# Three edits in an attention kernel: the causal mask of the row maxima, v's scale, v's low part

## The chip, the cores and the metric

The kernel runs on one core of a Trainium2 chip. The metric is the device time of one execution in microseconds. Three executions of the kernel before took 941.6, 941.88 and 940.47 us; the median is 941.6.

## The reference

Three parts follow each other. The sizes are 4 batches, 8 heads, 576 positions and 64 columns a head; the model width is 512.

```
# 1: attention with decay, per head
scores = q k^T / 8 + cum[i] - cum[j]          # cum: running sum of log f
scores[j > i] = -1e9;  scores -= max over j
attn = exp(scores);  attn /= sum + 1e-9
x = attn @ v                                  # heads side by side: 512 columns
# 2: low-rank mixing over positions, then a feed-forward block
u = x + (x^T @ U @ V)^T
x = u + relu(u @ w1) @ w2                     # w1 512x2048, w2 2048x512
# 3: four attention experts, the best two of each position weighted
logits = x @ w_gate;  w = softmax of the two largest, 0 for the others
out = sum over e of w[e] * (causal_softmax(x wq[e] (x wk[e])^T / 8) @ (x wv[e])) @ wo[e]
```

## The kernel before

Keys lie on the 128 partitions of a score tile and queries on its columns, so the row maximum cannot be had from that tile. The maxima are computed beforehand by matmuls of their own (`row_max`, one call per head): "ua" holds the last 128 queries against all 576 keys, "ub" the other four query tiles against the 64, 192, 320 and 448 keys that they may see. The last 128 keys of each (64 in the smallest) are the diagonal block, where the causal mask has to be applied: VectorE adds the mask tile maskm and takes the maximum in one operation per query tile (lines 158 and 176), in place in PSUM. The four operations of ub need all four of its matmuls, which stand together. The five columns are transposed on TensorE ("mt", line 181), shifted ("mr", line 183) and sent by two DMAs of the SP queue into row 66 of qa, from where the score matmuls subtract them.

`scores` makes the score tiles in three-term precision (qa with ka, qb with kb) and masks the diagonal blocks on TensorE: identb times maskt is added to the bank (the last matmuls of line 212). ScalarE takes the exponential (pf, line 221) and its fp16 part ph (line 222), VectorE the rest pl (line 223). `weighted_values` multiplies ph and pl with v's high part vh and low part vl; a column of constants beside vh gives the row sums, and `row_scales` divides.

v needs a scale before it is split in two fp16 parts. `value_scale` takes the largest absolute value of each partition on VectorE (am, line 250), then the largest of all partitions by a transpose on TensorE (amt) and a reduce (ar, line 255), keeps its power of two (two small operations), and sends it back to all partitions by a product with ones (rsp) and a reciprocal (rs, line 264). It is a generator: its callers place its pieces among other work. `value_parts` multiplies v in place on VectorE (vr, line 269), casts it to vh on ScalarE (line 270) and subtracts on GpSimd to get vl (line 271). The tile vr is loaded again two pairs later.

The program's order: the 32 heads of part 1 are 16 pairs. Pairs 0 to 3 (batch 0) run without other matmuls beside them, up to about 90 us. From pair 5 on, between about 120 and 420 us, every turn of a pair also takes some groups of the feed-forward matmuls of batches already done (GROUPS: 6, 6, 7, then 8 a pair). From 420 to 711 us the rest of the feed-forward runs alone. From 711 us on come the experts: 16 heads in four batches, with the projections of the next batch beside them. In a turn of pair p stand the scores of p, the maxima and v's scale of pair p + 1, and the loads of pair p + 2. The order on TensorE is written out by hand; the other engines' orders come from the framework, which simulates a timeline. SP's DMA queue is in order. w1 and w2 come in quarters through `narrow` (lines 307 to 310, VectorE and ScalarE) and a subtraction on GpSimd (line 345); GpSimd also makes the low parts of q and k (qb and kb, lines 519 to 522) and of u (ul, line 356). In part 3, `gates` (eq, gt, gex and others, VectorE) is put behind the instruction that `value_parts` returns.

Maxima of pair 0 are made at the start, and those of pair p + 1 in the turn of pair p; the 14 heads of pairs 0 to 6 have their ua between 11.6 and 154.6 us.

Of the kernel before, what the change touches and what calls it, by code (L numbers as in the profile page):

```python
# [8 lines left out]
F32 = mybir.dt.float32  # L9
# [8 lines left out]
P = 128  # L18
# [13 lines left out]
AUG = 67  # L32
NH2A = 2
# [25 lines left out]
def kernel(  # L59
# [51 lines left out]
    ones1 = const.tile([1, P], BF16, name="ones1")  # L111
    nc.gpsimd.memset(ones1[:], 1.0)
# [37 lines left out]
    def row_max(hb, mx, apart=False):  # L150
# [4 lines left out]
        for c0, c1 in ((0, HC), (HC, S)):  # L155
            nc.tensor.matmul(ua[:, c0 // HC, 0:HC], qa[0:66, M_LO[4]:S], ka[0:66, c0:c1],  # L156
                             start=True, stop=True)
        nc.vector.tensor_tensor_reduce(
            ua[:, :, 0:HC], ua[:, :, 0:HC],
            maskm[:].rearrange("p (c n) -> p c n", c=2), 1.0, NEG, OP.add, OP.max, mx[:, 4:5])  # L160
# [4 lines left out]
        for t in (3, 2, 1, 0):  # L165
            bk, off = where[t]
            w = M_W[t]
            n = 64 if t == 0 else P
            nc.tensor.matmul(ub[0:n, bk, off:off + w], qa[0:66, M_LO[t]:M_LO[t] + n],  # L169
                             ka[0:66, 0:w], start=True, stop=True)  # L170
        for t in (3, 2, 1, 0):
            bk, off = where[t]
            w = M_W[t]
            n = 64 if t == 0 else P
            m0 = S - P if t == 0 else S - w
            nc.vector.tensor_tensor_reduce(  # L176
                ub[0:n, bk, off:off + w], ub[0:n, bk, off:off + w], maskm[0:n, m0:m0 + w], 1.0, NEG,
                OP.add, OP.max, mx[0:n, t:t + 1])
# [68 lines left out]
    def value_scale(vr):  # L247

        am = small.tile([P, 1], F32, name="am")
        nc.vector.tensor_reduce(am[:], vr, AX.XYZ, OP.max, apply_absolute_value=True)  # L250
        yield
        at_ = psf.tile([1, P], F32, name="amt", tag="f")
        nc.tensor.transpose(at_[:], am[:], ident[:])
        ar = small.tile([1, 1], F32, name="ar")
        nc.vector.tensor_reduce(ar[:], at_[:], AX.X, OP.max)
        nc.vector.tensor_scalar(ar[:], ar[:], 1.0e-30, None, OP.max)
        nc.vector.tensor_scalar(ar[:].bitcast(I32), ar[:].bitcast(I32), 0x7F800000, None,
                                OP.bitwise_and)
        yield

        rp = psf.tile([P, 1], F32, name="rsp", tag="f")
        nc.tensor.matmul(rp[:], ones1[:], ar[:].bitcast(BF16)[:, 1:2], start=True, stop=True)
        rs = small.tile([P, 1], F32, name="rs")
        nc.vector.reciprocal(rs[:], rp[:])
        return rs

    def value_parts(vr, rs, vh, vl):

        scaled = nc.vector.tensor_scalar(vr, vr, rs[:, 0:1], VEXP, OP.mult, OP.mult)
        nc.scalar.copy(vh[:, :, :, 0:64], vr)  # L270
        nc.gpsimd.tensor_tensor(vl[:], vr, vh[:, :, :, 0:64], OP.subtract)
        return scaled

    def row_scales(av, rs, extra=None):
# [3 lines left out]
                                1.0e-9 * PSCALE * VEXP, rs[:, 0:1], OP.add, OP.mult)  # L278
# [192 lines left out]
    for i in range(2):  # L471
        vh_ = hpool.tile([P, 2, NT, 65], F16, name=f"vh{i}")
        vl_ = hpool.tile([P, 2, NT, 64], F16, name=f"vl{i}")
        nc.gpsimd.memset(vh_[:, :, :, 64:65], VEXP)
        vhs.append((vh_, vl_))
# [55 lines left out]
    def maxima(p, j, apart=False):  # L531
        if p < NPAIR:
            yield from row_max(pair_heads(p)[j], next_mx(), apart)
# [347 lines left out]
    def expert_values(b, y):  # L881
# [18 lines left out]
        nc.gpsimd.memset(vh[:, :, :, 64:65], VEXP)  # L900
# [213 lines left out]
```

## Time and profile before

| | |
|---|---|
| median of 3 executions | 941.6 us (940.47 to 941.88) |
| profiled execution, first to last instruction (span) | 939.0 us |
| TensorE busy | 847.3 us, 90% |
| VectorE busy | 562.3 us, 60% |
| ScalarE busy | 415.3 us, 44% |
| GpSimd busy | 294.1 us, 31% |
| mean granted clock of TensorE | 0.954 |

The span is that of one profiled execution; the page gives no time before its first and behind its last instruction. PE is TensorE, PEld its weight loads, DVE VectorE, ACT ScalarE, POOL GpSimd, SP the queue that issues most DMAs. L176 is line 176. A line such as "ub<-ub,maskm 128x448" names the output, the inputs and the shape (partitions x columns). "Idle before" is time in which the engine stood still ahead of such instructions, with what ended it. The granted clock is a share of full speed: 1.0 is 2.4 GHz, 0.5 is 1.2 GHz.

### The profile page before, as it was taken

Reading aid. Unit: us, or ns where it says so; the run is one execution under the profiler, and the core shown is the slowest. Engines: PE = TensorE matmul, PEld = TensorE weight load, DVE = VectorE, ACT = ScalarE, POOL = GpSimd, SP = SyncE. Lnnn points to the kernel's source line nnn. Section 1 sums busy time; section 2 is a strip of 40 time slices with the busy share of each in tenths; the row PEclk is TensorE's granted clock in tenths of the full one; section 3 lists DMA queues with packets and bytes.
Section 4 is the critical chain, followed back from the end, with each engine's and each line's share of the span. In section 5 each row is a group of like instructions: output and inputs, shape, how many; then the busy total and the mean of one; then the engine's idle time right before and its main releaser. Section 6 shows DMA issues by size and latency. Waiting matters only on the chain.

```text
span 939.0 us, 18998 instructions
## 1 busy us (share of the span) xinstructions
PE 847.3 (90%) x7480; PEld 792.6 (84%) x7480; DVE 562.3 (60%) x1468; ACT 415.3 (44%) x808; POOL 294.1 (31%) x262
## 2 busy tenths in 40 slices
PE   2886878999899989989998999999999897989897
PEld 2775767888899989989998999999999797978675
DVE  6798588787576657632256652222225778786653
ACT  4675546564445463332233342222113464644553
POOL 8545354353423333012135433323014131210100
PEclk9998567999999999999999999999999998989998
DMA  6345545353433341103178753424114130311222
GB/s 190 106 108 163 141 149 166 112 146 114 126 109 86 111 136 47 39 15 114 53 267 262 233 185 113 152 74 121 37 29 124 39 90 17 91 29 27 70 85 69
DMA packets 68777, 101.94 MB, mean 109 GB/s; under 512 B 6608, under 2 KB 49424, under 8 KB 68688
## 3 DMA queue, kind: packets, MB, share of 16 engines
q1 hardware_dynamic: 64416, 92.47, 33.4%
q10 hardware_dynamic: 4272, 8.26, 2.5%
q8 instruction: 59, 0.97, 0.4%
q14 instruction: 30, 0.25, 0.1%
HBM read 60.33 MB, written 22.56 MB: 88 GB/s over the span
## 4 chain that ended last, share of the span: by engine, by line
PE 70%; DVE 14%; DMA 6%; ACT 5%; issue 3%; POOL 1%; SPq 1%; POOLq 0%; ACTq 0%; DVEq 0%
PE cps L385 19%; PE hps L370 19%; PE sc L212 8%; PE pq L849 4%; PE po L935 3%; PE pv L892 3%; PE av L239 3%; DVE pl L223 2%; DMA ust<-udram 2%; PE ub L169 2%; DVE ub L176 2%; PE gp L552 2%; PE av L243 2%; PE av L241 2%; PE ua L156 1%
## 5 line engine op out<-in xcount | busy, mean ns | idle before, releaser
L385 PE MATMUL cps<-hh,w2h 128*128 128x288 f32 x512 | 155.4, 304 | 6.8 <-DVE yc L387 3.8
L223 DVE TENSOR_TENSOR pl<-pf,ph 128x576 f16<-128x576 f32 x144 | 121.6, 847 | 54.4 <-ACT ph L222 54.2
L385 PE MATMUL cps<-hh,w2l 128*128 128x288 f32 x512 | 152.2, 297 | 1.0 <-POOL w2l L345 1.0
L370 PE MATMUL hps<-uh,w1h 128*128 128x288 f32 x512 | 145.2, 305 | 6.7 <-ACT uh L355 6.7
L385 PE MATMUL cps<-hl,w2h 128*128 128x288 f32 x512 | 151.2, 295 | 0.0
L370 PE MATMUL hps<-uh,w1l 128*128 128x288 f32 x512 | 141.9, 299 | 0.0
L375 DVE SCALAR_TENSOR_TENSOR hl<-hps,hh 128x288 fp32r<-128x288 f32 x128 | 58.2, 455 | 127.3 <-ACT hh L374 127.1
L374 ACT ACTIVATE hh<-hps 128x288 fp32r<-128x288 f32 x128 | 52.3, 409 | 168.6 <-PE hps L370 168.4
L221 ACT ACTIVATE pf<-sc 128x576 f32<-128x576 f32 x144 | 83.6, 612 | 52.3 <-PE sc L212 48.6
L385 PEld LDWEIGHTS cps<-hh,w2h 128*128 128x128 f32 x512 | 97.1, 190 | 8.3 <-DVE yc L387 4.5
L370 PEld LDWEIGHTS hps<-uh,w1h 128*128 128x128 f32 x512 | 97.9, 191 | 7.2 <-ACT uh L355 7.2
L370 PEld LDWEIGHTS hps<-uh,w1l 128*128 128x128 f32 x512 | 98.0, 191 | 0.0
L385 PEld LDWEIGHTS cps<-hh,w2l 128*128 128x128 f32 x512 | 96.9, 189 | 1.2 <-POOL w2l L345 1.2
L385 PEld LDWEIGHTS cps<-hl,w2h 128*128 128x128 f32 x512 | 96.9, 189 | 0.0
L370 PE MATMUL hps<-ul,w1h 128*128 128x288 f32 x512 | 89.6, 297 | 3.2 <-POOL ul L356 3.2
L212 PE MATMUL sc<-qa,ka 67*128 67x288 f32 (+4 forms) x288 | 79.1, 334 | 14.6 <-DMA qa<-mr 5.5
L222 ACT CAST ph<-pf 128x576 f16<-128x576 f32 x144 | 88.7, 638 | 1.6
L239 PE MATMUL av<-vh,ph 128*128 128x65 f16 x720 | 86.4, 202 | 1.5 <-DVE x L286 1.5
L176 DVE CUSTOM_DVE_ANT_0 ub<-ub,maskm 128x448 f32<-128x448 f32 x192 | 81.4, 424 | 7.2 <-PE ub L169 6.0
L241 PE MATMUL av<-vl,ph 128*128 128x64 f16 x720 | 85.1, 198 | 0.0
L243 PE MATMUL av<-vh,pl 128*128 128x65 f16 x720 | 84.8, 198 | 0.0
L356 POOL TENSOR_TENSOR ul<-ust,uh 128x1152 fp32r<-128x1152 f32 x22 | 58.8, 2671 | 80.9 <-ACT uh L355 80.9
(160 smaller groups left out, 1984.9 us busy)
## 6 DMA issues: line engine op xcount, KB each, us to landing
raw<-in_w_dram SPq DMA_DIRECT2D x32, 512.0 KB
ust<-udram SPq DMA_DIRECT2D x22, 576.0 KB
qkt<-in_qk_dram SPq DMA_DIRECT2D x16, 576.0 KB
yc<-ydram SPq DMA_DIRECT2D x14, 576.0 KB
ydram<-yc SPq DMA_DIRECT2D x14, 576.0 KB
vr<-in_v_dram SPq DMA_DIRECT2D x16, 320.0 KB
udram<-ustage ACTq DMA_DIRECT2D x16, 288.0 KB
ydram<-ust SPq DMA_DIRECT2D x8, 576.0 KB
```

The source lines that it names most:

```text
L176: nc.vector.tensor_tensor_reduce(ub[0:n, bk, off:off + w], ub[0:n, bk, off:off + w], maskm[0:n, m0:m0 + w], 1.0, NEG, OP.add, OP.max, mx[0 ...
L212: nc.tensor.matmul(ps[:, bk, off:off + w], wa, xa, start=bk not in banks[:n], stop=bk not in banks[n + 1:])
L221: nc.scalar.activation(pfv, view, AF.Exp, scale=ISC)
L222: nc.scalar.copy(ph[:, o0:o0 + n], pf[:, 0:n])
L223: nc.vector.tensor_tensor(pl[:, o0:o0 + n], pf[:, 0:n], ph[:, o0:o0 + n], OP.subtract)
L239: nc.tensor.matmul(av[0:m, it, :], ph[0:k, c:c + m], vh[0:k, jt, :], start=first, stop=False)
L241: nc.tensor.matmul(av[0:m, it, 0:64], ph[0:k, c:c + m], vl[0:k, jt, :], start=False, stop=False)
L243: nc.tensor.matmul(av[0:m, it, :], pl[0:k, c:c + m], vh[0:k, jt, :], start=False, stop=last)
L356: nc.gpsimd.tensor_tensor(ul[:], ust[:], f32(uh[:]), OP.subtract)
L370: nc.tensor.matmul(ph[:], wa[:, k, fs], xa[:, k, :], start=n == 0, stop=n == 3 * KT - 1)
L375: nc.vector.scalar_tensor_tensor(hl[:], ph[:], 0.0, f32(hh[:]), OP.max, OP.subtract)
L385: nc.tensor.matmul(pc[:], wa[:, t, dsl], xa[:], start=n == 0, stop=n == 3 * FT - 1)
```

## The change

For the heads of pairs 0 to 6 (PLAIN = 7) the mask of the maxima is added on TensorE: identb times the diagonal columns of maskm, one matmul for ua and four for ub, behind the products in the same bank; VectorE then takes a plain maximum of each query tile. The other heads, those of part 3 too, keep the fused operation.

v's scale is one product: the partition maxima, now bf16, with a 128x128 tile of ones. Their sum over the partitions stands in for the largest of them; VectorE scales it by 1/8192, takes the power of two and the reciprocal. The column of constants beside vh is 1.0 and no longer 8192.

v is no longer scaled in place: ScalarE multiplies by rs and casts in one pass, and vl is one VectorE operation, v times rs minus vh. `value_parts` returns this last operation.

```diff
@@ -30,6 +30,7 @@
 NQ = 4
 FT = FF // P // NQ
 AUG = 67
+PLAIN = 7
 NH2A = 2
 NH2B = 4
 PSCALE_LN = 8.0 * math.log(2.0)
@@ -108,8 +109,8 @@
                             compare_op=OP.is_ge, fill=BIG, base=0, channel_multiplier=1)
 
 
-    ones1 = const.tile([1, P], BF16, name="ones1")
-    nc.gpsimd.memset(ones1[:], 1.0)
+    every = const.tile([P, P], BF16, name="every")
+    nc.gpsimd.memset(every[:], 1.0)
 
     def make_heads(pl_, n, decay):
 
@@ -147,17 +148,22 @@
             except StopIteration as end:
                 return end.value
 
-    def row_max(hb, mx, apart=False):
+    def row_max(hb, mx, apart=False, onpe=False):
 
 
         qa, qb, ka, kb = hb
         ua = ps2.tile([P, 2, 512], F32, name="ua", tag="s2")
         for c0, c1 in ((0, HC), (HC, S)):
             nc.tensor.matmul(ua[:, c0 // HC, 0:HC], qa[0:66, M_LO[4]:S], ka[0:66, c0:c1],
-                             start=True, stop=True)
-        nc.vector.tensor_tensor_reduce(
-            ua[:, :, 0:HC], ua[:, :, 0:HC],
-            maskm[:].rearrange("p (c n) -> p c n", c=2), 1.0, NEG, OP.add, OP.max, mx[:, 4:5])
+                             start=True, stop=c0 == 0 or not onpe)
+        if onpe:
+            nc.tensor.matmul(ua[:, 1, HC - P:HC], identb[:], maskm[:, S - P:S], start=False,
+                             stop=True)
+            nc.vector.tensor_reduce(mx[:, 4:5], ua[:, :, 0:HC], AX.XY, OP.max)
+        else:
+            nc.vector.tensor_tensor_reduce(
+                ua[:, :, 0:HC], ua[:, :, 0:HC],
+                maskm[:].rearrange("p (c n) -> p c n", c=2), 1.0, NEG, OP.add, OP.max, mx[:, 4:5])
         if apart:
             yield
         ub = ps2.tile([P, 2, 512], F32, name="ub", tag="s2")
@@ -167,12 +173,21 @@
             w = M_W[t]
             n = 64 if t == 0 else P
             nc.tensor.matmul(ub[0:n, bk, off:off + w], qa[0:66, M_LO[t]:M_LO[t] + n],
-                             ka[0:66, 0:w], start=True, stop=True)
+                             ka[0:66, 0:w], start=not onpe or t > 1, stop=not onpe)
+        for t in (0, 3, 2, 1) if onpe else ():
+            bk, off = where[t]
+            n = 64 if t == 0 else P
+            off += M_W[t] - n
+            nc.tensor.matmul(ub[0:n, bk, off:off + n], identb[0:n, 0:n],
+                             maskm[0:n, S - P:S - P + n], start=False, stop=t in (1, 3))
         for t in (3, 2, 1, 0):
             bk, off = where[t]
             w = M_W[t]
             n = 64 if t == 0 else P
             m0 = S - P if t == 0 else S - w
+            if onpe:
+                nc.vector.tensor_reduce(mx[0:n, t:t + 1], ub[0:n, bk, off:off + w], AX.X, OP.max)
+                continue
             nc.vector.tensor_tensor_reduce(
                 ub[0:n, bk, off:off + w], ub[0:n, bk, off:off + w], maskm[0:n, m0:m0 + w], 1.0, NEG,
                 OP.add, OP.max, mx[0:n, t:t + 1])
@@ -246,36 +261,30 @@
 
     def value_scale(vr):
 
-        am = small.tile([P, 1], F32, name="am")
+        am = small.tile([P, 1], BF16, name="am")
         nc.vector.tensor_reduce(am[:], vr, AX.XYZ, OP.max, apply_absolute_value=True)
         yield
-        at_ = psf.tile([1, P], F32, name="amt", tag="f")
-        nc.tensor.transpose(at_[:], am[:], ident[:])
-        ar = small.tile([1, 1], F32, name="ar")
-        nc.vector.tensor_reduce(ar[:], at_[:], AX.X, OP.max)
-        nc.vector.tensor_scalar(ar[:], ar[:], 1.0e-30, None, OP.max)
-        nc.vector.tensor_scalar(ar[:].bitcast(I32), ar[:].bitcast(I32), 0x7F800000, None,
+        sp = psf.tile([P, 1], F32, name="rsp", tag="f")
+        nc.tensor.matmul(sp[:], every[:], am[:], start=True, stop=True)
+        rs = small.tile([P, 1], F32, name="rs")
+        nc.vector.tensor_scalar(rs[:], sp[:], 1.0 / VEXP, 1.0e-30, OP.mult, OP.max)
+        nc.vector.tensor_scalar(rs[:].bitcast(I32), rs[:].bitcast(I32), 0x7F800000, None,
                                 OP.bitwise_and)
+        nc.vector.reciprocal(rs[:], rs[:])
         yield
-
-        rp = psf.tile([P, 1], F32, name="rsp", tag="f")
-        nc.tensor.matmul(rp[:], ones1[:], ar[:].bitcast(BF16)[:, 1:2], start=True, stop=True)
-        rs = small.tile([P, 1], F32, name="rs")
-        nc.vector.reciprocal(rs[:], rp[:])
         return rs
 
     def value_parts(vr, rs, vh, vl):
 
-        scaled = nc.vector.tensor_scalar(vr, vr, rs[:, 0:1], VEXP, OP.mult, OP.mult)
-        nc.scalar.copy(vh[:, :, :, 0:64], vr)
-        nc.gpsimd.tensor_tensor(vl[:], vr, vh[:, :, :, 0:64], OP.subtract)
-        return scaled
+        nc.scalar.mul(vh[:, :, :, 0:64], vr, rs[:, 0:1])
+        return nc.vector.scalar_tensor_tensor(vl[:], vr, rs[:, 0:1], vh[:, :, :, 0:64], OP.mult,
+                                              OP.subtract)
 
     def row_scales(av, rs, extra=None):
 
         den = small.tile([P, NT], F32, name="den")
         nc.vector.tensor_scalar(den[:], av[:, :, 64:65].rearrange("p t o -> p (t o)"),
-                                1.0e-9 * PSCALE * VEXP, rs[:, 0:1], OP.add, OP.mult)
+                                1.0e-9 * PSCALE, rs[:, 0:1], OP.add, OP.mult)
         rn = small.tile([P, NT], F32, name="rn")
         nc.vector.reciprocal(rn[:], den[:])
         if extra is not None:
@@ -471,7 +480,7 @@
     for i in range(2):
         vh_ = hpool.tile([P, 2, NT, 65], F16, name=f"vh{i}")
         vl_ = hpool.tile([P, 2, NT, 64], F16, name=f"vl{i}")
-        nc.gpsimd.memset(vh_[:, :, :, 64:65], VEXP)
+        nc.gpsimd.memset(vh_[:, :, :, 64:65], 1.0)
         vhs.append((vh_, vl_))
     NPAIR = B * NP
     st_in, st_rs, st_p = {}, {}, {}
@@ -530,7 +539,7 @@
 
     def maxima(p, j, apart=False):
         if p < NPAIR:
-            yield from row_max(pair_heads(p)[j], next_mx(), apart)
+            yield from row_max(pair_heads(p)[j], next_mx(), apart, p < PLAIN)
 
     def one(gen):
 
@@ -897,7 +906,7 @@
                 yield
         vh = sy.tile([P, NT, E, 65], F16, name="vh3")
         vl = sy.tile([P, NT, E, 64], F16, name="vl3")
-        nc.gpsimd.memset(vh[:, :, :, 64:65], VEXP)
+        nc.gpsimd.memset(vh[:, :, :, 64:65], 1.0)
         vv_ = vr[:, :, 0:E * D].rearrange("p t (e d) -> p t e d", e=E)
         scale = value_scale(vv_)
         next(scale)
```

## Rows read from the trace of the kernel before

**Rows 1.** Each engine's busy us in four stretches: A:B, length, engines, clock, DMA

```profile
0.00:160.00 160.00, 114.72 (x979) 99.32 (x980) 123.25 (x320) 91.04 (x162) 85.47 (x88) 0.83 0.50 144
87.00:132.00 45.00, 32.83 (x200) 28.34 (x201) 29.43 (x62) 21.16 (x38) 21.31 (x13) 0.51 0.51 155
160.00:420.00 260.00, 247.05 (x2476) 228.63 (x2474) 172.88 (x482) 128.98 (x246) 87.21 (x64) 0.98 0.33 97
711.00:939.00 228.00, 199.32 (x1884) 179.57 (x1882) 155.68 (x445) 116.23 (x248) 32.98 (x36) 0.95 0.23 61
```

**Rows 2.** Chain of waits, 0 to 160 us: shares of 160 us by line

```profile
by line: PE sc L212 14.0%; issue 9.9%; DVE pl L223 6.6%; DMA qa<-mr 4.6%; DVE wst L307 4.5%; DVE ub L176 4.5%; ACT pf L221 3.8%; PE ub L169 3.7%; DMA qkt<-in_qk_dram 2.9%; ACT ph L222 2.7%; PE av L239 2.7%; PE gp L552 2.5%; DVE ua L158 2.4%
```

**Rows 3.** Chain of waits, 711 to 939 us: shares of 228 us

```profile
by line: PE pq L849 16.6%; PE po L935 12.8%; PE sc L212 10.4%; PE pv L892 10.4%; DVE pl L223 3.8%; DVE ub L176 3.4%; PE av L239 3.4%; DVE am L250 2.6%; PE ub L169 2.6%; PE av L243 2.2%; PE av L241 2.2%; DMA yst<-ydram 2.0%; DVE eq L819 2.0%
```

**Rows 4.** TensorE in order of time near 44 and 50 us: start, us

```profile
43.95 0.58 PE L212 MATMUL sc<-maskt,identb 128*128 128x64 bf16 x4
44.32 0.42 PE L181 MATMUL mt<-ident,mx 128*5 128x128 f32 x1
...
50.48 0.37 PE L212 MATMUL sc<-maskt,identb 128*128 128x64 bf16 x4
50.69 0.27 PE L181 MATMUL mt<-ident,mx 128*5 128x128 f32 x1
```

**Rows 5.** Groups by line, 0 to 160 us: busy us, mean ns, idle before

```profile
L176 DVE CUSTOM_DVE_ANT_0 ub<-ub,maskm 128x448 f32<-128x448 f32 (+3 forms) x56 | 23.8, 425 | 3.4 <-PE ub L169 3.0
...
L169 PE MATMUL ub<-ka,qa 66*128 66x448 f32 (+3 forms) x56 | 13.7, 384 | 3.8 <-DVE mx L158 3.1 <-ACT pf L221 0.7
...
L158 DVE CUSTOM_DVE_ANT_0 ua<-ua,maskm 128x576 f32<-128x576 f32 x14 | 10.6, 759 | 5.5 <-PE ua L156 5.5
...
L176 DVE DVE_READ_ACCUMULATOR2_ANT mx<- 128x1 f32 (+1 forms) x56 | 7.6, 136 | 0.0
...
L250 DVE TENSOR_REDUCE am<-vr 128x1 f32<-128x640 f32 x7 | 5.7, 810 | 3.0 <-DMA vr<-in_v_dram 3.0
...
L270 ACT CAST vh<-vr 128x640 f16<-128x640 f32 x7 | 5.1, 727 | 4.3 <-DVE vr L269 4.3
...
L269 DVE TENSOR_SCALAR vr<-vr,rs 128x640 f32<-128x640 f32 x7 | 4.3, 621 | 0.0
...
L255 DVE TENSOR_REDUCE ar<-amt 1x1 f32<-1x128 f32 x7 | 1.9, 273 | 1.3 <-PE amt L253 1.3
```

**Rows 6.** Line 309 of the whole span: shortest, median, longest ns

```profile
L309 DVE SCALAR_TENSOR_TENSOR wst<-raw,wst x32: 675/693/2699, 76.4 to 560.0; 128x512 int32<-128x512 int32 x32
```

**Rows 7.** VectorE, GpSimd and TensorE in order of time, 83 to 92 us

```profile
86.92 1.83 DVE L223 TENSOR_TENSOR pl<-pf,ph 128x512 f16<-128x512 f32 x1
...
88.81 1.75 DVE L309 SCALAR_TENSOR_TENSOR wst<-raw,wst 128x512 int32<-128x512 int32 x1
...
86.79 1.41 POOL L271 TENSOR_TENSOR vl<-vr,vh 128x640 f16<-128x640 f32 x1
88.28 1.73 POOL L522 TENSOR_TENSOR kb<-qkt,kb 64x576 fp32r<-64x576 f32 x1
...
91.03 0.58 PE L561 MATMUL up<-vs,g 96*128 96x256 f32 x1 [7.21 <-DVE g L556]
```

**Rows 8.** VectorE and TensorE in order of time, 777 to 784 us

```profile
777.40 1.01 DVE L269 TENSOR_SCALAR vr<-vr,rs 128x1280 f32<-128x1280 f32 x1
...
780.32 2.56 DVE L819 TENSOR_TENSOR eq<-eq,tie 128x80 f32<-128x80 f32 x1
...
783.22 0.38 PE L181 MATMUL mt<-ident,mx 128*5 128x128 f32 x1 [5.21 <-DVE rn L280]
```

**Rows 9.** VectorE's groups by line, 711 to 939 us

```profile
L819 DVE TENSOR_TENSOR eq<-eq,tie 128x80 f32<-128x80 f32 x4 | 5.0, 1246 | 0.0
...
L821 DVE TENSOR_TENSOR gt<-gt,eq 128x80 f32<-128x80 f32 x4 | 3.0, 742 | 0.0
L830 DVE SCALAR_TENSOR_TENSOR gex<-rank,gex 128x20 f32<-128x20 f32 x4 | 2.6, 653 | 0.1
```

## The prediction, made before the change was run

> **What bounds the kernel now.** I read the busy times by stretch first, then the chain of waits of each stretch, then single lines. The stretches [rows 1] tell three kernels apart. Up to 160 us no engine is full: TensorE 115, VectorE 123, ScalarE 91, GpSimd 85 of 160 us. From 160 to 420 us TensorE has 247 of 260: the feed-forward matmuls fill every gap. From 711 us on, the expert attention, TensorE has 199 of 228 and VectorE 156. The feed-forward stretch between (420 to 711) holds none of the changed code. So a saving on VectorE or GpSimd is worth something before 160 and after 711, and a matmul costs its full time between 160 and 420. The change adds matmuls for pairs 0 to 6 only, and the maxima of pair 6 are issued in the turn of pair 5, so all 14 heads lie before 160 us.
>
> The chain before 160 us is mixed [rows 2]: scores on TensorE 14.0%, pl on VectorE 6.6%, the maxima's VectorE lines 4.5% (ub) and 2.4% (ua), their TensorE line ub 3.7%. In the last stage [rows 3] TensorE leads, but "eq", a 128x80 compare in the gates, holds 2.0% of 228 us, 4.6 us: far too much for 80 columns. That is the row to chase.
>
> I make the sum against the profiled execution's span of 939.0 us. The page gives no time around it; the median of the three runs, 941.6, is 2.6 above, and I carry those 2.6 over unchanged.
>
> **Maxima: TensorE pays.** Each of the 14 heads gets five more bf16 matmuls: four for ub (64 and three times 128 columns) and one of 128 for ua. The scores already do the same four with the same identity [rows 4]. From the first of them to the next instruction is 0.37 us at 44 us and 0.21 us at 50 us; the ua one is 128/448 of that. So 0.48 us a head at the lower clock, 0.27 at the higher. Eight of the 14 heads' maxima fall in lower-clock time (five before 46 us, two between 87 and 132 us, where the granted clock is 0.51 [rows 1], one near 155 us), six at the higher: 3.8 + 1.6 = 5.5 us. On the path: the line ub of TensorE is 3.7% of 160 us, 5.9 us, out of 13.7 busy [rows 2, 5], that is 43%. I take **+2.4**; ends 0 (all hidden in TensorE's idle time) and +5.5.
>
> **Maxima: VectorE.** Before, a head costs 0.759 + 4 x 0.425 = 2.46 us, and five accumulator reads of 0.136 [rows 5]. No plain max-reduce of these widths is in the trace; the nearest are "am", 640 columns in 0.810, and "ar", 128 from PSUM in 0.273 [rows 5]. A line through them is 0.139 us + 1.05 ns a column, so 1600 columns in five reduces are 2.37 us: 0.09 less. In the timeline the next instruction mostly starts together with the read, so the read costs its time only between two neighbouring maxima. I take 0.25 us a head, 3.5 us in all, nearer to 1.2 (reads free) than to 10.7 (reads paid in full). About a third of such work is on the path (ub 7.2 of 23.8 us, ua 3.8 of 10.6 [rows 2, 5]): **-1.1**, ends -0.4 and -3.6.
>
> **v's scale.** The transpose, the max over 128, max, and, product, reciprocal become one product, one fused multiply and max, and, reciprocal: on VectorE the 0.273 reduce goes, three small ones stay three. TensorE loses an instruction. Seven sets before 160 us, a third on the path: **-0.6**. The new product waits for the same am as the old transpose did; behind it on TensorE wait the same matmuls.
>
> **v's low part.** On GpSimd the subtraction vl goes. What it did to VectorE stands at 87 us [rows 7]: pl took 1.83 us while vl ran from 86.79 to 88.20; wst, after it, took 1.75 while GpSimd's kb ran from 88.28 to 90.01; behind both stood g, for which TensorE sat idle 7.21 us. The VectorE instruction ends only after the GpSimd one does. Without vl, kb starts 1.4 us earlier and one stall of 1.75 - 0.69 = 1.06 us goes (0.69 is that line's median [rows 6]). There is one more such place, near 119.7 us, which I price alike: together **-2.1**. VectorE gets in exchange a two-source operation for its scaling: by wst [rows 6] 0.675 for 512 columns and 1.05 ns for each further one make 0.81 for 640, against 0.62 [rows 5]: 0.19 x 7, a third of it, **+0.4**. Like pl it reads two SBUF tensors, so it can itself stand behind a GpSimd subtraction: GpSimd is busy for 85 of 160 us [rows 1], so about every second one does, for half of kb's 1.73 us on average: 0.45 x 7, a third of it, **+0.9** (ends 0 and 7 x 1.73 us, all on the path, +12). ScalarE scales in the pass in which it casts: 0.73 us stays 0.73, cost nothing; if it became a tenth longer, 0.07 us a set. On SP's queue the load of v two pairs on waits for vr's last reader, and the rows of ka, qb and kb stand behind it; that reader is now done about half a microsecond sooner (0.81 against 1.41 us), or later by as long as the new operation waits. I price it at nothing, the first rival holds its bad end.
>
> The Trainium skill, page "SBUF — State Buffer", section "Who interferes with whom", says that a VectorE instruction with two SBUF inputs contends with a GpSimd one that reads SBUF, and that the later of the two blocks fully. It speaks against this edit, and rows 7 agree with it. Left out, the sum below would be -7.1; with it, -6.2.
>
> On the rate of the operation, rule and row differ. The Trainium skill, page "Vector Engine (DVE) Microarchitecture Reference", section "Points that are easy to get wrong", has the throughput of this operation's form halved when both tensors come from SBUF and neither is bf16, as vr and vh do. The row shows 512 columns of two int32 SBUF tensors in 0.675 us [rows 6]. By the row the sum is -6.2; by the rule it is the last rival.
>
> **Middle stretch.** Nine sets of scale and low part beside a TensorE that is 95% busy [rows 1]: the 13 idle us can shrink a little: **-0.5**, ends -2 and +2.
>
> **Last stage.** Four sets of 1280 columns. By the line above a 128x80 operation costs 0.22 us and a 128x20 one 0.16. The gates' eq, gt and gex average 1.246, 0.742 and 0.653 over four [rows 9]: 4.1 + 2.1 + 2.0 = 8.2 us of stalls, one in each set, each while vl ran. At 780.32 the eq took 2.56 and the last reduce of the maxima stood behind it, so that TensorE sat idle for 5.21 us until 783.22 [rows 8]. I count three sets of four on the path (gex's is in one set, where nothing waits): 6.2 us gone. The new operation is 0.675 + 768 x 1.05 ns = 1.48 against 1.00 (rows 8 show 1.01), +0.48 x 3; ar -0.27 x 3. Together **-5.6**; ends 0 (the next late operation, such as ScalarE's exp, takes it all) and -10 (the 5.21 us gap closes almost whole).
>
> **Sum**: 2.4 - 1.1 - 0.6 - 2.1 + 0.4 + 0.9 - 0.5 - 5.6 = -6.2. Span 932.8, time **935.4 us**.
>
> **Rivals.**
> VectorE waits for ScalarE (slower). Before, GpSimd waited for vh and nobody waited for GpSimd. Now the low part stands in VectorE's own order, and behind it pl, the maxima's reduces and hl. Standing directly behind the reciprocal, it waits a whole vh: 0.73 us in 16 sets [rows 5], about twice that in four: 17.5 us. For it: the vh of the trace mostly starts just as the scaling ends. Against: the order has other work to put between. It turns the sign from 6.2 us on the path, 35% of those waits; with two thirds, +11.7 - 6.2 = +5.5: 947 us.
> The gain is off the path (same). All 5.5 us of the masks count and the last stage gives only half: -6.2 + 3.1 + 2.8 = -0.3, 941.3 us. For it: ub's TensorE line feeds the reduce directly. Against: the 5.21 us gap.
> The clock comes back early (faster still). From 87 to 132 us the granted clock is 0.51 [rows 1], after the 7.21 us gap of TensorE [rows 7]. If that gap shrank enough, half of the stretch's 32.8 TensorE us would go; two thirds of that on the path give 11 us: 924.4 us. Against: I take only 1.06 us out of that gap.
> Half rate of the new operation: 1.05 ns more per column makes 0.67 x 16 + 1.34 x 4 = 16 us on VectorE, a third on the path: +5.4 - 6.2 = -0.8, 940.8 us. Against it: the wst row. This is the rule of the Trainium skill's page "Vector Engine (DVE) Microarchitecture Reference", cited above.
>
> **How the numbers follow.** Forecast 0.55 (its own range 931 to 939.5), waiting VectorE 0.15, off the path 0.16, clock 0.09, half rate 0.05. The range of 8 in 10 reaches from the clock's middle to the near half of the slower case: **926 to 944.5**. A measurement of this kernel tells 0.2%, 1.9 us, from no change. Faster by more than that, under 939.7: forecast 0.53, clock 0.09, a third of the off-path case: **0.67**. Within: half of the off-path case, most of half rate, the forecast's edge: **0.15**. Slower: the waiting VectorE and the rest of the off-path case: **0.18**.
>
> **What would show it.** Right: no vl on GpSimd; eq, gt, gex near 0.2 us; TensorE's gap before 783 us about half; reduces of 0.75 us for 576 columns without accumulator reads; 14 x 5 bf16 matmuls more. Wrong: idle VectorE time in front of vl ended by ScalarE's vh (first rival); vl at 1.5 us for 640 columns (half rate); TensorE's wait before the maxima's reduces longer than the masks' 0.37 us. The prediction fails if the stretch up to 160 us grows by over 3 us, or if the one from 711 us on shrinks by less than 3.

## The result: slower, and where the time went

The changed kernel takes 950.0 us (median of 7 executions, 947.1 to 953.8) against 941.6 (7 executions, 940.3 to 947.4): ratio 1.0091, 95% interval 1.0064 to 1.0118. Forecast were 935.4 us and a range of 926 to 944.5; the forecast was wrong, in sign too. The profiled execution's span is 949.6 us against 939.0, its granted clock 0.948 against 0.954. Executions of one kernel scatter, in the runs below over 3 to 17 us, and each kernel has one trace: a stretch that differs by a few microseconds between two traces need not differ between the kernels. Busy us, share of the span and instructions of each engine:

```profile
PE 853.1 (90%) x7530; PEld 800.5 (84%) x7530; DVE 551.9 (58%) x1378; ACT 416.2 (44%) x808; POOL 258.9 (27%) x242
```

VectorE has 10.4 us less than before and GpSimd 35.2, TensorE 5.8 more.

Lines are numbered anew: old L176 is L189 (L191 for the heads that keep the fused operation), L169 L175, L158 L162 (L164), L250 L265, L309 L318, L819 L828, L821 L830, L830 L839, L212 L227, L181 L196; the masks are L160 and L181, vh L279, vl L280, the product with ones L268.

To lay the two traces side by side I cut both where the same x of the attention (the normalised output of one head) is written, and at the first mr of the experts. Kernel before, then after; columns as in [rows 1]:

```profile
42.60:70.00 27.40, 24.40 (x302) 21.73 (x301) 24.22 (x80) 19.66 (x36) 11.71 (x9) 1.00 0.38 105
...
105.00:158.50 53.50, 42.98 (x314) 37.44 (x315) 39.94 (x92) 27.88 (x51) 24.85 (x16) 0.66 0.46 141
...
212.50:235.90 23.40, 21.71 (x222) 19.68 (x222) 17.22 (x53) 11.73 (x23) 8.26 (x6) 1.00 0.42 123
235.90:416.90 181.00, 173.12 (x1750) 160.72 (x1749) 111.93 (x315) 84.78 (x161) 53.99 (x43) 0.98 0.29 85
...
729.30:939.00 209.70, 182.56 (x1759) 163.28 (x1757) 143.81 (x413) 106.66 (x222) 26.28 (x26) 0.95 0.21 57
```

```profile
43.50:78.10 34.60, 31.74 (x311) 28.29 (x310) 21.64 (x57) 19.88 (x35) 9.84 (x7) 0.67 0.31 81
...
112.40:169.00 56.60, 41.11 (x362) 36.90 (x363) 40.06 (x76) 28.55 (x53) 22.81 (x14) 0.82 0.45 135
...
221.00:252.30 31.30, 26.76 (x238) 24.45 (x238) 20.35 (x55) 13.67 (x27) 8.37 (x6) 0.85 0.43 130
252.30:436.80 184.50, 173.25 (x1749) 160.78 (x1748) 113.43 (x309) 84.85 (x161) 45.89 (x36) 0.98 0.27 81
...
749.00:949.60 200.60, 178.84 (x1755) 161.07 (x1753) 136.25 (x409) 107.46 (x222) 14.33 (x22) 0.97 0.21 59
```

The last stage gains 9.1 us, as its part of the change was meant to (forecast 5.6). The 20 us lost before it lie in four places (21.7 together; the stretches left out give 2 back). Near 43 us: +7.2, with TensorE idle for 2.9 us instead of 3.0; nearly all of it is busy time at a lower granted clock (0.67 for 1.00). Near 112 us: +3.1, with 48 more matmuls and idle 15.5 us instead of 10.5. Near 221 us: +7.9, 2.8 of it idle and the rest busy time, with 16 more matmuls and again a lower clock. From 252 us on: +3.5, nearly all idle. Of the waits of TensorE, those that grew (us in total, times, longest): first 0 to 165 us, before and then after; then 170 us to the end of the attention, before and then after:

```profile
PE sc L212 <- DMA qa<-mr: 5.5, 4, 3.1
PE hps L370 <- ACT uh L355: 4.2, 1, 4.2
```

```profile
PE hps L379 <- ACT uh L364: 8.7, 1, 8.7
PE sc L227 <- DMA qa<-mr: 7.9, 5, 3.1
```

```profile
PE up L561 <- DVE mr L183: 0.6, 1, 0.6
```

```profile
PE up L570 <- DVE mr L198: 5.8, 7, 1.0
...
PE cps L394 <- ACT w2h L353: 2.8, 1, 2.8
```

None of these waits ends on an edited operation; where one could be followed back, it comes from an order that the framework had planned anew. The first wait for uh stands on SP's queue, before and then after (start, us, what is issued):

```profile
118.21 1.27 SPq L352 DMA_DIRECT2D ust<-udram  x2
119.58 0.56 SPq L487 DMA_DIRECT2D qkt<-in_qk_dram  x1
121.00 0.33 SPq L489 DMA_DIRECT2D vr<-in_v_dram  x1
```

```profile
117.06 0.54 SPq L498 DMA_DIRECT2D vr<-in_v_dram  x1
117.69 0.47 SPq L524 DMA_DIRECT2D ka<-kb  x1
118.25 0.55 SPq L527 DMA_DIRECT2D kb<-kb  x1
...
125.09 0.33 SPq L496 DMA_DIRECT2D qkt<-in_qk_dram  x1
125.52 1.27 SPq L361 DMA_DIRECT2D ust<-udram  x2
```

After the change the load of qkt goes first and holds the queue until GpSimd has read the last qkt (its kb, 123.66 us plus 1.40); both loads of u (ust, from which ScalarE makes uh) stand behind it. The load of v has moved too: ahead of the row copies ka and kb, where it stood behind them.

The waits for mr from 252 us on stand on VectorE, after and then before:

```profile
296.30 0.87 DVE L280 SCALAR_TENSOR_TENSOR vl<-vr,rs,vh 128x640 f16<-128x640 f32 x1
297.20 0.28 DVE L565 TENSOR_TENSOR g<-gp,g 32x128 fp32r<-32x128 f32 x1
300.18 0.82 DVE L265 TENSOR_REDUCE am<-vr 128x1 bf16<-128x640 f32 x1 [2.70 <-DMA vr<-in_v_dram]
301.04 0.28 DVE L198 TENSOR_SCALAR mr<-mt 5x128 fp32r<-5x128 f32 x1
```

```profile
295.55 0.82 DVE L250 TENSOR_REDUCE am<-vr 128x1 f32<-128x640 f32 x1 [0.73 <-DMA vr<-in_v_dram]
297.02 0.28 DVE L183 TENSOR_SCALAR mr<-mt 5x128 fp32r<-5x128 f32 x1 [0.66 <-PE mt L181]
```

After the change am stands between g and an mr that does not need it, waits 2.70 us for v, and TensorE's second up waits 0.98 us behind both. In the kernel before am comes half a turn later, behind the mr that follows g and ahead of the turn's other one (297.02). Only the first four pairs have two tiles vr; from pair 4 on there is one, and the load of v for the next pair waits for the low part vl of this one. It is issued as vl, now on VectorE, ends (296.30 plus 0.87):

```profile
297.20 0.34 SPq L498 DMA_DIRECT2D vr<-in_v_dram  x1
```

### The profile page after: what moved, and what is told of

Its sections match the earlier page's. It is cut to its first block, busy times and chain, and to the rows that moved or that the text cites. A ratio compares the mean times of both kernels' runs of the same rounds, so it can differ in the third digit from the quotient of the medians.

```text
span 949.6 us, 18987 instructions
## 1 busy us (share of the span) xinstructions
PE 853.1 (90%) x7530; PEld 800.5 (84%) x7530; DVE 551.9 (58%) x1378; ACT 416.2 (44%) x808; POOL 258.9 (27%) x242
## 4 chain that ended last, share of the span: by engine, by line
PE 66%; DVE 14%; DMA 9%; ACT 5%; issue 3%; POOL 1%; SPq 1%; ACTq 0%; POOLq 0%; DVEq 0%
PE cps L394 19%; PE hps L379 18%; PE sc L227 8%; PE pq L858 4%; DVE pl L238 3%; PE po L944 3%; DMA ust<-udram 3%; PE av L254 2%; PE pv L901 2%; PE ub L175 2%; DMA qa<-mr 2%; PE av L258 2%; PE av L256 2%; ACT pf L236 2%; DMA vr<-in_v_dram 2%
## 5 line engine op out<-in xcount | busy, mean ns | idle before, releaser
L379 PE MATMUL hps<-uh,w1h 128*128 128x288 f32 x512 | 147.1, 308 | 10.3 <-ACT uh L364 10.3
L238 DVE TENSOR_TENSOR pl<-pf,ph 128x576 f16<-128x576 f32 x144 | 116.1, 809 | 52.1 <-ACT ph L237 51.4
L379 PE MATMUL hps<-uh,w1l 128*128 128x288 f32 x512 | 143.8, 302 | 0.0
L379 PEld LDWEIGHTS hps<-uh,w1h 128*128 128x128 f32 x512 | 99.4, 194 | 10.8 <-ACT uh L364 10.8
L227 PE MATMUL sc<-qa,ka 67*128 67x288 f32 (+4 forms) x288 | 78.4, 333 | 21.4 <-DMA qa<-mr 11.1
L254 PE MATMUL av<-vh,ph 128*128 128x65 f16 x720 | 89.4, 205 | 1.5 <-DVE x L295 1.5
L256 PE MATMUL av<-vl,ph 128*128 128x64 f16 x720 | 88.0, 201 | 0.0
L258 PE MATMUL av<-vh,pl 128*128 128x65 f16 x720 | 87.7, 200 | 0.0
L379 PEld LDWEIGHTS hps<-ul,w1h 128*128 128x128 f32 x512 | 77.2, 192 | 4.1 <-POOL ul L365 4.1
```

The costliest lines, as they stand in the source:

```text
L227: nc.tensor.matmul(ps[:, bk, off:off + w], wa, xa, start=bk not in banks[:n], stop=bk not in banks[n + 1:])
L238: nc.vector.tensor_tensor(pl[:, o0:o0 + n], pf[:, 0:n], ph[:, o0:o0 + n], OP.subtract)
L254: nc.tensor.matmul(av[0:m, it, :], ph[0:k, c:c + m], vh[0:k, jt, :], start=first, stop=False)
L256: nc.tensor.matmul(av[0:m, it, 0:64], ph[0:k, c:c + m], vl[0:k, jt, :], start=False, stop=False)
L258: nc.tensor.matmul(av[0:m, it, :], pl[0:k, c:c + m], vh[0:k, jt, :], start=False, stop=last)
L379: nc.tensor.matmul(ph[:], wa[:, k, fs], xa[:, k, :], start=n == 0, stop=n == 3 * KT - 1)
```

## The experiments

Each kernel ran on a chip with the kernel before; the ratio's 95% interval stands in brackets. The medians of the kernel before were 939.1 to 942.0 us on these chips, so runs from different chips are best compared by their ratios.

**Parts of the change.** Run 1, the values without the masks:

```
-PLAIN = 7
+PLAIN = 0
```

> The change without its masks (PLAIN 0, so the row maxima are masked on VectorE as before); the edits of v's scale and low part stay. Theory A, the masks on TensorE make the loss of some 20 us up to 420 us, and the gain of some 9 us behind 711 us is the values': 941.6 - 9 = about 932. Theory B, the low part in VectorE's order makes the loss (the load of vr waits for it, VectorE's am waits 20.6 us for that load where it waited 9.9): about 950, as the whole change. Half way, 941, would say that each has a part.

939.6 us [0.9927 to 0.9983]: between the two theories. The attention ends at 426.4 us (before 416.9, after 436.8) and the last stage gains its 9 us.

Run 2, the kernel before with `row_max` of the change and nothing else:

```
-            yield from row_max(pair_heads(p)[j], next_mx(), apart)
+            yield from row_max(pair_heads(p)[j], next_mx(), apart, p < PLAIN)
```

> The kernel before with nothing but the masks of the first seven pairs on TensorE. Theory A: the loss of 20 us without the gain of 9, about 960. Theory B: 941 to 944 (the prediction's +2.4 and -1.1).

936.4 us [0.9911 to 0.9967]: faster. Theory A falls: the masks by themselves cost nothing.

Run 3, the kernel before with `value_scale` and `value_parts` of the change (here with _x) in `expert_values` alone:

```
-        scale = value_scale(vv_)
+        scale = value_scale_x(vv_)
...
-        with tc.issue_after(value_parts(vv_, rs, vh, vl).ins):
+        with tc.issue_after(value_parts_x(vv_, rs, vh, vl).ins):
```

> The kernel before with the new scale and low part in the expert attention alone. Both theories: the stretch up to 711 us as before, the last stage 9 us shorter, about 932; eq, gt and gex near 0.2 us. If the 9 us of the whole change came from something else (the clock, the order), about 938 to 942.

933.2 us [0.9878 to 0.9951]: as both theories had it. The experts start at 728.9 us, as before; the last stage takes 201.5 us instead of 209.7.

Run 4, the scale alone; against run 1:

```
-        nc.scalar.mul(vh..., vr, rs[:, 0:1])
-        return nc.vector.scalar_tensor_tensor(vl[:], vr, rs[:, 0:1], vh...)
+        scaled = nc.vector.tensor_scalar(vr, vr, rs[:, 0:1], None, OP.mult)
+        nc.scalar.copy(vh[:, :, :, 0:64], vr)
+        nc.gpsimd.tensor_tensor(vl[:], vr, vh[:, :, :, 0:64], OP.subtract)
+        return scaled
```

> The kernel before with the scale from one product with ones and nothing else: v is scaled in place on VectorE, the low part stays on GpSimd, the masks on VectorE. Theories A and B: 940 to 942, since the scale costs a few small instructions (the prediction's -0.6), and the stalls of eq, gt and gex beside GpSimd's low part stay as they were.

951.3 us [1.0062 to 1.012]. The edit that both theories took for free costs 9 us, as much as the whole change loses. Its operations are fewer than before. What it changes besides is the place of the product: the old scale took two places in TensorE's order (transpose, then product, one step of the generator apart); the new one has its only product where the transpose stood. The step is less than a turn of a pair: one head later for pairs 0 to 3, behind the next head's maxima from pair 4 on. v's next load comes one head earlier with it, and what the framework plans around both is planned anew.

**The place of the product.** Run 5, the change with am held behind mr:

```
-            one(vals)
+            with tc.issue_after(cur["mr"].ins):
+                one(vals)
```

> The whole change, with v's absolute maximum am of the attention's later pairs held behind the maxima's mr in VectorE's order (in the whole change it stands ahead of one, waits there for the load of vr, and TensorE's second up waits behind: 7 times, 5.8 us; in the kernel before am stands behind that mr). Theory C, what the change costs up to 420 us comes from places that instructions take in an engine's order: the seven waits go, 950 - 6 = 944. Theory D, these waits are only where an already late chain shows: the time stays at 950 and other waits take their place.

950.1 us [1.0059 to 1.0176]. Of the seven waits for mr one is left, from 170 us on, as in the kernel before (the line below); the time stays: as theory D had it for this wait.

```profile
PE up L570 <- DVE mr L198: 0.6, 1, 0.6
```

Run 6, the change with the product one step later (a `yield` more ahead of it, one less behind):

```
         nc.vector.tensor_reduce(am[:], vr, ...)
         yield
+        yield
         sp = psf.tile([P, 1], F32, name="rsp", tag="f")
```

> The whole change, with the product with ones moved back to the place in TensorE's order where the second of the old products stood (the third step of v's scale, behind the next maxima's mt). Theory C: v's parts are made as late as before, so that vr, am and the weights' narrowing fall into the old places, and 10 to 18 of the 20 us come back: 932 to 940. Theory D, the work itself (low part on VectorE, masks on TensorE) costs the time: 947 to 952.

931.8 us [0.9877 to 0.9924]. With all operations of the change in it, 18 us come back: theory C.

Run 7, runs 2 and 3 together; against run 3:

```
-            yield from row_max(pair_heads(p)[j], next_mx(), apart)
+            yield from row_max(pair_heads(p)[j], next_mx(), apart, p < PLAIN)
```

> The masks of the first seven pairs on TensorE and the new scale and low part in the expert attention only; the attention's scale and low part as before. If the two parts add (masks alone 941.96 to 936.4, experts alone to 933.2): 941.96 - 5.5 - 8.7 = 927.7. If the masks' gain was one of order and chance, 930 to 934.

932.2 us [0.9864 to 0.992]: between the sum of the parts and the second forecast. Beside run 3 the masks bring 1 us by the medians and 2 by the ratios, where they brought 5.5 alone; the intervals are too wide to tell whether the parts add.

Run 8, run 4 with the later product of run 6; against run 4:

```
         yield
+        yield
         sp = psf.tile([P, 1], F32, name="rsp", tag="f")
```

> The scale from one product with ones and nothing else, but with the product at the old place of the second product (third step). Theory C, the earlier product costs the 9 us of the run with the scale alone (951.3): 941 to 943. Theory D, the operations of the new scale cost it: 949 to 952.

930.1 us [0.9841 to 0.9895]. By its place alone the same product costs 9 us or gains 10 to 12 (medians against the kernel before, and ratio). Of the 16.7 us between the two traces 10.8 lie in the attention and 5.8 in the last stage.

**Which order.** Run 9, the change with the load of v at the start of `values` (a part of the edit):

```
+        if vr is None:
+            with tc.issue_after(cur["last"].ins):
+                vr = load_v(p)
```

> The whole change, TensorE's order untouched, but each pair's load of v is issued behind the last rows mr on SP's queue, as the reading of v begins. (In the whole change the load stands in the middle of the row copies of ka, qb and kb and ahead of mr's rows; in the kernel before and with the product at the third step it stands behind them.) Theory C1, the load's place on that queue is what the early product costs: 10 us or more of the 18 come back, 932 to 940. Theory C2, the place on VectorE and ScalarE of v's own work costs it, or the clock after the waits: 946 to 952.

956.4 us [1.0111 to 1.0213]: slower, but the edit missed its aim. The load came so late that TensorE now waits for am:

```profile
PE rsp L268 <- DVE am L265: 19.8, 6, 5.8
```

It tells nothing for C2; it does not bear C1 out either.

Run 10, against run 8:

```
-PLAIN = 0
+PLAIN = 7
```

> The masks on TensorE and the scale from one product, the product at the third step, the low part on GpSimd everywhere. If the scale at the third step (930.1) and the masks (-5.5) add: 924 to 925. If both draw on the same slack: 929 to 932, and the masks are worth nothing here.

941.1 us [0.9984 to 1.0047]: neither. Here the masks cost 11 us (14 by the ratios), although the product has its late place.

Run 11, against run 6:

```
-PLAIN = 7
+PLAIN = 0
```

> The scale from one product at the third step and the low part on VectorE, masks on VectorE as before. Beside the scale at the third step with the low part on GpSimd (930.1) this prices the low part's move by itself: the prediction's +0.4, +0.9, -2.1 and most of the last stage's -5.6 make -5, 925; if the last stage's gain came with the product's place already, 928 to 931; if the low part in VectorE's order costs, 933 to 937.

931.7 us [0.987 to 0.9945]. The low part's move by itself is worth nothing that these runs can tell (930.1 without it), and the masks nothing beside it (931.8 with them). Run 11 is also run 1 with the product one step later: 931.7 for 939.6 us, 8 us by the medians and 5 by the ratios. Without the masks the same step is worth less than half of what runs 4 and 6 show.

Run 12, the change's `value_parts` (with _x) in `expert_values`; against run 10:

```
-        with tc.issue_after(value_parts(vv_, rs, vh, vl).ins):
+        with tc.issue_after(value_parts_x(vv_, rs, vh, vl).ins):
```

> As the run with the masks and the scale at the third step, and the low part on VectorE in the expert attention only. The stalls of eq, gt and gex beside GpSimd's low part go: 2 to 6 us under that run, 919 to 928. If the third step has taken the low part out of their way already: the same as that run.

939.1 us [0.9931 to 1.0011]: 2 us under run 10, within the noise of both.

**Orders by themselves.** So the masks gave -5.5 (run 2), -1 (run 7), +10 (run 1 against the change), +11 (run 10) and 0 us (run 11 against run 6), by what stood beside them. Runs 13 to 16 add next to no work:

```
+            for _ in range(NULL if u == 0 and "fu" not in cur else 0):
+                nc.tensor.matmul(ps[:, 0, 0:64], identb[:], maskm[:, 0:64], start=True, stop=True)
```

Run 13, before, NULL = 1:

> The kernel before with one 64-column matmul more ahead of each of the first batch's eight score blocks, its result overwritten: work of about 8 x 0.1 us. It also moves the orders that the framework plans for the other engines (168 lines of VectorE's, 25 of SP's); on SP's queue the load of qkt now stands ahead of the first ust. Theory E, the orders that fall out of the plan decide and not the work of an edit: the time moves by far more than 1 us, and with qkt ahead of ust TensorE's first wait for uh is 8 us or more where it was 4.2: 944 to 952. Theory F, the work decides: 941 to 943, the wait for uh as before.

Run 14, before, NULL = 2:

> As the run before, with two such matmuls (some 1.6 us of work at most); again qkt ahead of ust on SP's queue, elsewhere another order. Theory E: away from 942 by several us, first wait for uh 8 us or more: 944 to 952. Theory F: 942 to 944.

Run 15, after, NULL = 1:

> The whole change with one such matmul ahead of each of the eight score blocks. On SP's queue both ust loads now stand ahead of qkt; the load of v stays early. Theory E: TensorE's first wait for uh falls from 8.7 to about 4.5 us, and the time moves by several us, to 940 to 946. Theory F: 950 to 952.

Run 16, after, NULL = 2:

> The whole change with two such matmuls; qkt stands ahead of ust as in the whole change. Theory E: the wait for uh stays at 8 us or more, the rest can fall either way: 943 to 957. Theory F: 950 to 953.

Measured 940.6 [0.9953 to 1.0002], 946.9 [1.0034 to 1.0097], 944.8 [1.001 to 1.006] and 950.9 us [1.0052 to 1.0127]. The traces have these matmuls ahead of ten score blocks and not eight, since the two heads of pair 4 get them too: ten with NULL = 1, 2.2 us of busy time, and twenty with NULL = 2, 2.6 us. This much work moves the kernel before by +5 (run 14) and the changed one by -5 (run 15); in runs 13 and 16 the time stays within 1.4 us. The wait for uh follows the queue as forecast, in run 13 (qkt first) and run 15 (ust first):

```profile
PE hps L373 <- ACT uh L358: 8.1, 1, 8.1
```

```profile
PE hps L382 <- ACT uh L367: 4.8, 1, 4.8
```

Over all 20 kernels: with ust first this wait is 3.9 to 4.9 us (11 kernels), with qkt first 5.9 to 10.7 (9 kernels). But run 13, with the longer wait, kept its time, against theory E: no single wait carries the total. Runs 14 and 15 moved as theory E had it and not as F; run 16 fits both. Three draws on either kernel (NULL 0, 1 and 2) spread over some 6 us, and do not bridge the 18 to 21 us between runs 4 and 8 or between the change and run 6. The 5 to 8 us between runs 1 and 11 they could.

**The last stage on other heads.** Run 17, the same edit against run 8:

```
-        with tc.issue_after(value_parts(vv_, rs, vh, vl).ins):
+        with tc.issue_after(value_parts_x(vv_, rs, vh, vl).ins):
```

> The scale from one product at the third step everywhere, the low part on VectorE in the expert attention only, masks on VectorE. Up to 711 us the orders are those of the scale alone at the third step (930.1); the last stage was 193.1 us there and 188 to 189.5 in the runs with that step and the low part on VectorE. If the last stage's gain is one of its own edits and does not hang on the orders before it: 930.1 - 4 = 926. If it is one more draw of the orders: 930 to 940.

930.5 us [0.9831 to 0.9925]: nothing gained on run 8. Run 18, the experts' product one step later; against run 7, in `value_scale_x`:

```
         yield
+        yield
         sp = psf.tile([P, 1], F32, name="rsp", tag="f")
```

> The masks on TensorE, the attention's scale and low part as in the kernel before, the experts' scale at the third step with the low part on VectorE. Up to 711 us the orders are those of the run with the masks and the experts' values (932.2), whose last stage was 193.7 us: 932.2 - 4 to 5 = 927 to 928 if the last stage's gain stands by itself, 932 to 937 if not.

931.1 us [0.982 to 0.9927]. In the profiles the stage from the experts' first mr takes 202.1 us in run 17 (202.7 in run 8) and 199.0 in run 18 (203.4 in run 7): next to none where the later place had already brought the gain. The 4.4 us of run 18 are not sure: its trace is of its fastest execution (922.7 us), and its median is 1 us under run 7. Runs 8, 17 and 18 beat the kernel before by 1.2 to 1.3% and cannot be told apart.

## Why the prediction was wrong

By its own test it failed in the stretch up to 160 us: the x written there at 158.5 us comes at 169.0, 10.5 later, where it allowed 3. The middle stretch, to the last x, grew by another 9.4 where it had -0.5.

**The step that failed** is the one on v's scale, with its companion on SP's queue. The prediction said of the new product that "behind it on TensorE wait the same matmuls", took -0.6 us for the instructions saved, and priced the earlier release of v "at nothing". All three look at the operations and hold the orders fixed. But the product's place decides when v can be scaled and when its buffer comes free: the eighth load of v is issued after the 10th x in the changed kernel and runs 1 and 4, after the 11th in the kernel before and runs 6, 8, 10 and 11. What stands around it on VectorE, ScalarE, GpSimd and SP's queue is planned anew with it. Moving the product alone is worth 18 us of the change's own time (run 6), 21 beside the scale alone (runs 4 and 8), and 5 to 8 without the masks (runs 1 and 11). No term of the sum stood for it, and none of the rivals.

How the place becomes time is not shown. Without the waits behind am the time stayed (run 5), the edit on the load missed its aim (run 9), and the order of ust and qkt does not follow the place: in runs 4 and 8 alike ust goes first.

**Masks on TensorE** (+2.4, VectorE -1.1). The operations have the sizes forecast, but the time that they cost, -5.5 to +11 us in five pairs of runs, is not the +1.3 of the two terms. The maxima as plain reduces, and the masks, 0 to 170 us:

```profile
L189 DVE TENSOR_REDUCE mx<-ub 128x1 f32<-128x448 f32 (+3 forms) x56 | 19.9, 412 | 8.5 <-PE ub L181 7.3 <-PE rsp L268 1.2
...
L162 DVE TENSOR_REDUCE mx<-ua 128x1 f32<-128x576 f32 x14 | 10.5, 749 | 4.8 <-PE ua L160 4.7
```

749 and 412 ns against 759 and 425 [rows 5], the accumulator reads gone. VectorE's idle time ahead of ub's reduces grew from 3.4 to 8.5 us, 0.36 us a head: about the masks' own 0.37, so the sign that I had named for wrong, a wait longer than that, does not show. Runs 2 and 11 say that the masks can gain or be free; run 1 against the change (10 us) and run 8 against run 10 (11 us) say that this depends on the order that they meet. How their matmuls lead to the longer waits, step by step, was not settled.

**The low part** (-2.1, +0.4, +0.9; by a third on the path the last is 1.0). The operation came out as sized:

```profile
L280 DVE SCALAR_TENSOR_TENSOR vl<-vr,rs,vh x20: 871/880/1890, 12.8 to 872.5; 128x640 f16<-128x640 f32 x16, 128x1280 f16<-128x1280 f32 x4
...
  ACT vh L279: 1.8, 4
```

Shortest, median and longest ns; below, VectorE's idle time ahead of it: 1.8 us in 20 operations. So the slower rival (VectorE waits for vh) and the half rate both fall: 0.88 us for 640 columns, where I had 0.81 and the half rate 1.48. The Trainium skill, "Vector Engine (DVE) Microarchitecture Reference", section "Points that are easy to get wrong", halves this form's throughput; the trace does not show that. Up to 170 us the mean is 1207 ns: three of the seven began beside a subtraction of GpSimd and took 1.78, 1.89 and 1.27 us, each ending 0.7 us behind it; the other four took 0.87 to 0.88. That is 2.3 us in all (I had 3.2). The rule that a VectorE instruction with two SBUF inputs contends with a GpSimd one that reads SBUF, in the Trainium skill's "SBUF — State Buffer", section "Who interferes with whom", agrees with this, and its price here is small. Of the -2.1, TensorE's wait for g near 91 us shows a part: 7.2 us before, 5.6 after.

**The last stage** (-5.6, measured -9.1). The stalls are gone as forecast, 0.23, 0.23 and 0.17 us for 1.25, 0.74 and 0.65 [rows 9]:

```profile
L828 DVE TENSOR_TENSOR eq<-eq,tie 128x80 f32<-128x80 f32 x4 | 0.9, 226 | 0.0
L830 DVE TENSOR_TENSOR gt<-gt,eq 128x80 f32<-128x80 f32 x4 | 0.9, 227 | 0.1
L839 DVE SCALAR_TENSOR_TENSOR gex<-rank,gex 128x20 f32<-128x20 f32 x4 | 0.7, 167 | 0.1
```

TensorE's idle time in the stage falls from 27.1 to 21.8 us, its busy time by 3.7 at a clock of 0.97 for 0.95; the clock I had not counted. The 5.21 us gap [rows 8] is gone whole; one of 2.7 us behind the third set has become 3.4. At the change's place of the product the low part's move carries this gain: the stage takes 208.6 us in run 4, without it, and 200.3 in run 1, with it. What I had not seen is the larger wait beside it, in both kernels the same; before and after, from 727 us on:

```profile
PE amt L253 <- DVE am L250: 5.7, 4, 2.0
PE mt L181 <- DVE rn L280: 5.2, 1, 5.2
```

```profile
PE rsp L268 <- DVE am L265: 5.4, 4, 2.0
PE mt L196 <- DVE rn L291: 4.4, 2, 3.4
```

With the later place the product no longer waits for am, in none of the four sets; run 8 gains 7.0 us in this stage (202.7) with GpSimd's low part and its stalls still there (eq averages 1.37 us). So the gain can be had in two ways, which don't add (run 17).

**The clock.** I had a rival in which it rises early. In the changed kernel it fell instead, 0.67 from 43.5 to 78.1 us, where the kernel before had 1.00; behind that it stood higher than before (0.82 for 0.66 near 112 us). It is not the masks' doing as such; run 18 has them and stays at the higher level, run 15 does not:

```profile
42.00:68.70 26.70, 24.13 (x318) 20.70 (x316) 23.45 (x60) 19.66 (x36) 12.98 (x9) 1.00 0.40 109
```

```profile
43.30:78.10 34.80, 32.28 (x312) 28.77 (x313) 21.74 (x57) 19.77 (x35) 9.86 (x8) 0.66 0.31 82
```

Nearly the same work, 2.6 and 2.5 us idle, 8 us apart. Why the level fell in one and not in the other is open, and it need not be the orders. Runs 10 and 12 differ in the expert attention only, and up to 78 us VectorE, ScalarE and SP's queue have the same operations in the same order; yet their traces show the same stretch 3.3 us apart at two clocks:

```profile
41.83:73.92 32.09, 26.32 (x316) 23.13 (x315) 25.57 (x57) 19.88 (x36) 15.04 (x10) 0.89 0.32 85
```

```profile
42.39:77.77 35.38, 31.76 (x315) 28.42 (x315) 23.93 (x58) 19.54 (x35) 14.03 (x10) 0.81 0.33 89
```

So a part of the 7.2 us near 43 us can belong to the execution that was traced and not to the change. The profile's 1.00 also needs care up to 46 us in the kernel before: av's matmuls take 245 ns there (20 to 46 us), as at 0.51 (90 to 130 us), and 197 from 50 to 86 us. The level was the lower one up to about 46 us, as the prediction had read it.

**The range** ended at 944.5 because it was built from the prices of operations. It lacked a term for the product's place, and, as runs 13 to 16 show, an uncertainty of some 5 us from the orders alone. It also took 0.2% as told from no change, where seven executions of the kernel before spread over 0.75% (940.3 to 947.4 us).

## What to carry over

Where a framework plans the engines' orders, the first question about an edit is not what its operations cost but whether it moves a product in the hand-written order, and what is released by it: here one `yield` was worth 5 to 21 us, and the same five matmuls a head between -5.5 and +11, each by what stood beside it. Before crediting an edit with a gain or loss under 1%, run it beside a null edit (here 2 us of work whose result is overwritten); if that moves the time as far, the edit has not been measured. In this case the last stage, in which TensorE leads, came out from its rows in sign and to 3.5 us; the stretch in which no engine is full did not.

## What the runs showed that I had not expected

Matmuls of 2.2 and 2.6 us in total moved the time by 5 us either way (runs 15 and 14). Two stretches with nearly the same work and the same idle time differ by 8 us through the granted clock (1.00 and 0.66), in one trace of each kernel. One wait, w2h near 220 us, goes with a slow stretch: the seven kernels in which it is 2.8 to 5.5 us take 31.0 to 33.4 us from the 15th to the 17th x, the other thirteen, in which it is at most 1.1 us, 22.5 to 26.0. The difference is more than the wait, and the clock is lower (0.85 in the changed kernel, 1.00 before). It is not shown that the wait lowers the clock: in the changed kernel, where the wait ends at 231.6 us, it is 0.50 from 220.2 to 223.6 us, ahead of the wait, and again from 230.5 to 237.2.
